# Attention, MoE and MLP in one kernel: token sums tied into the order, weight conversion shifted between blocks, one weight split and one set of weight sums placed elsewhere

## The chip, the cores and the metric

One Trainium2 chip, one core. The metric is the device time of one execution in microseconds; the kernel before takes 698.25 us (median of three runs, 697.82 to 699.86).

## The reference

Three stages follow each other on 1152 tokens of width 512 (2 batches of 576).

```python
scores = scale * q @ k.T + decay, causal          # 2 batches, 8 heads, head size 64
attn   = softmax(scores) @ v                      # -> x, 1152 x 512
p      = domain_probs / (sum + 1e-9)
out    = sum over 4 experts of p[:, e] * (relu(x @ w1[e]) @ w2[e])   # 512 -> 1024 -> 512
h      = out @ w_in;  g = h * sigmoid(1.702 * h)  # 512 -> 2048
result = g @ w_out                                # 2048 -> 512
```

All of it is float32; the MLP's two weights arrive as 64-bit floats.

## The kernel before, in words

**Precision.** Every operand of a product is split into a high part, rounded by ScalarE to the type that TensorE takes, and a low part, the remainder, subtracted by VectorE. A product is three matmuls: high by high, low by high, high by low. So each weight needs a split (`split_w`, line 242: ScalarE rounds on line 71 into `whi`, VectorE subtracts on line 249 into `wlo`), and each result is evacuated from PSUM with a rounding and a subtraction (`evac_l1`, lines 1082 to 1088; `output`, lines 980 to 985, in which VectorE makes `jc`, ScalarE applies relu and rounds to `hh`, and GpSimd subtracts `hl`).

**Units.** The experts are cut into 8 blocks of half an expert, the MLP into 4 blocks (8 to 11). `visits` lists which block is worked on when, over which groups of tokens; `seq` lists the units in order. A unit of kind 1 is a first layer (4 steps), kind 2 a second layer (one step for each tile of 128 tokens), kinds 4 and 5 a second layer of a visit without rest (8 and 2 steps), kinds 3 and 7 are joint first layers in 7 steps. While visits 0 to 6 run, attention is woven in: `pull()` emits a piece of it, and the number of pulls of a step is `n`, worked out from what is due and how many steps are left (line 1404). Visits 7 to 9 (`v_exp` to `v_all`) handle 640 of the tokens for three blocks; visit 10 is `v_all`; visits 11 to 13 (`both_joint`) handle all tokens, 640 of them (`EXP`) in joint units of 320 columns and the other 512 (`REST`) in joint units of 256 columns; visits 14 to 17 are the MLP.

**Joint units.** `emit_joint` (line 961) multiplies two halves of the tokens with two halves of the weights in 7 products of 6 matmuls in place of 8, after Strassen and Winograd. It needs sums of weights (`sum_weights`, line 260: four GpSimd operations on lines 270 to 273 into `sr`; `high_sums` and `low_sums` split them into `sh` and `sl`) and sums of tokens: `sum_tokens` (line 309) for EXP, and `rest_sums` (line 338) for the 512 tokens of REST. The last of the 7 products (s4) adds onto a bank that `third_out` reads first, on VectorE (line 980).

**Token sums of REST.** `rest_sums` is a generator of 44 steps: twice 22, for two halves of the width. 28 are VectorE operations of 128x256 (20 sums on line 362, 8 subtractions on line 355), 8 are ScalarE roundings, 8 are transfers (line 357) from the one buffer `rs` to DRAM. Its scratch lies in an attention pool. Three steps of it are emitted at each step of `seq` from the fourth step of unit (1, 5, 1, 1) on. They name only their data, so the scheduler puts them on the engines as early as these allow.

**Order.** A scheduler orders each engine's instructions by program order among those that are ready in its own estimate of time. `in_turn(fn)` (line 799) ties each instruction that fn emits to come behind the one emitted last on its engine (TensorE, VectorE, ScalarE and GpSimd; not SyncE, which issues most transfers). From visit 7 to 13 `pin_turn` fixes the emitted order on VectorE, ScalarE and GpSimd, and on TensorE where the line `pinned = ...` says so. In a step the order is: matmuls of the step, pulls, token sums, evacuation of the step before (`evac[0]()`), a split that is due, what `place()` puts at that step, conversion.

**place().** `put(u, g, what, ...)` (line 1283) puts an action at step g of unit u. For a visit of `both_joint` the units are, in order: h0 = (3, v, ., EXP[0]); the second layer of REST of the visit before; r0 = (7, v, ., 0); h1 = (3, v, ., EXP[1]); r1 = (7, v, ., 1); l2 = (2, v, ., EXP[0]). The four splits of the second layer's weights ("b") and the weight sums of the next visit are put there by hand.

**Conversion.** `mlp_convert` (line 406) turns an MLP weight from 64-bit to 32-bit floats in 6 steps of the generator: one VectorE operation of 128x512 each (lines 419, 422, 425, 428, 431, 433); the first has a ScalarE operation (line 418) ahead of it, the last is followed by a load (line 400) and a store (line 446) on SyncE. `cv_due` collects a rate at every step of `seq`, and each whole unit of it emits one step of the generator. There are 32 weights, 192 steps.

Of the kernel before, what the change touches and what calls it, by code (L numbers as in the profile page):

```python
# [28 lines left out]
EXP = [NCH + 3, NCH + 4, NCH + 5]  # L29
# [21 lines left out]
def attn_moe_mlp(ctx: ExitStack, tc: tile.TileContext, qk0, qk1, qk2, v0, vp, fg, dp, wa_moe, wb_moe, wa_mlp, wb_mlp, out):  # L51
# [36 lines left out]
    late = {}  # L88
# [67 lines left out]
    v_exp, v_all, v_mlp = len(visits), len(visits) + 3, len(visits) + 7  # L156
    visits += [(b, EXP[:2]) for b in (3, 1, 0)] + [(b, EXP) for b in range(4, NMOE)] + [(b, MLP) for b in range(NMOE, NBLK)]
    joint = [v_ for v_ in range(v_exp, len(visits)) if v_ != v_mlp]
    both_joint = range(v_all + 1, v_mlp)
# [616 lines left out]
    def in_turn(fn, *args):  # L776

        block = nc.cur_bb.bb.instructions
        n, prev = len(block), {}
        for i in block:  # L780
            prev[i.engine] = i
        fn(*args)
        for i in block[n:]:
            if i.engine in turn_engines:
                if i.engine in prev:
                    tc.add_manual_dep(i, prev[i.engine].name,
                                      mybir.DependencyInfo(mybir.DependencyClass.NoSync, mybir.DependencyReason.DATA),
                                      reason="in_turn")
                prev[i.engine] = i
# [496 lines left out]
    def place():  # L1286

        at = {}

        def put(u, g, what, *args):  # L1290
            at.setdefault((u, g), []).append((what, args))

        for v_ in range(v_exp, v_all):
            b, (c1, c2) = visits[v_]
            h0, h1, l2 = (3, v_, b, c1), (3, v_, b, c2), (4, v_, b, c1)
            put(h0, 1, sum_weights, v_ + 1, 0)
            put(h1, 1, sum_weights, v_ + 1, 1)
            for u, m in ((l2, 0), ((5, v_, b, c1), 1)):
                put(u, -0.5, high_sums, v_ + 1, m)
                put(u, 0, low_sums, v_ + 1, m)  # L1300
            first = v_ == v_exp
            places = [(h1, 5), (h1, 6)] + [(l2, i) for i in range(1, 7)]
            if first:
                put((6,) + units[-1], -0.5, high_sums, v_, 1)
                put((6,) + units[-1], 0, low_sums, v_, 1)
                nxt0 = (3, v_ + 1, visits[v_ + 1][0], c1)
                places = [(h0, 0), (h0, 1)] + places + [(nxt0, 0), (nxt0, 1)]
            todo = [("b", v_)] * first + [("a", v_ + 1), ("b", v_ + 1)]
            for (kind, w_, g), (u, i) in zip([(*t, g) for t in todo for g in range(4)], places):
                put(u, i, split_w, kind, w_, g)  # L1310
        for v_ in range(v_all, v_mlp):
            b, (c1, c2, _) = visits[v_]
            h0, h1, l2 = (3, v_, b, c1), (3, v_, b, c2), (2, v_, b, c1)
            more = v_ + 1 in both_joint
            if v_ == v_all:
                mid = (1, v_, b, REST)
                put(h1, 0, load_rest_sums)
                put(h0, 1, sum_weights, v_ + 1, 0)
                put(mid, -0.5, high_sums, v_ + 1, 0)
                put(mid, 0, low_sums, v_ + 1, 0)  # L1320
                put(mid, 1, sum_weights, v_ + 1, 1)
                continue
            r0, r1 = (7, v_, b, 0), (7, v_, b, 1)
            put(r0, -0.5, split_rest)
            put(r0, 5.5, high_sums, v_, 1)
            put(h1, -0.5, low_sums, v_, 1)
            if more:
                put((2, v_ - 1, b - 1, REST), 2, sum_weights, v_ + 1, 0)
                put(h1, 1, sum_weights, v_ + 1, 1)
                put(r1, 6, high_sums, v_ + 1, 0)  # L1330
                put(l2, 0, low_sums, v_ + 1, 0)
            fill = (2, v_ - 1, b - 1, REST)
            for k, (u, i) in enumerate([(fill, 3), (fill, 3), (r0, 1), (r1, 1)]):
                put(u, i, split_w, "b", v_, k)
            for g in range(4):
                put(l2, g, split_w, "a", v_ + 1, g)
        return at
# [11 lines left out]
    late_by = [3]  # L1349
    rest_gen, rest_from = [], seq.index((1,) + units[6])  # L1350
    cv_due = [0]
    in_turn(emit_first, 3, True)
    for i, (kind, v_, b, c) in enumerate(seq):
# [24 lines left out]
        for g in range(n_steps):  # L1378
            if kind in (2, 6):
                split_until("b", v_, range(4))  # L1380
            elif kind not in (4, 5):
                split_until("a", v_, [g] if kind == 1 else range(4))
            if i == 0:
                ev = lambda: None
            elif kind in (3, 7):
                ev = next(j_gen)
            else:
                if kind in (4, 5) and ("b", v_, 2 if kind == 5 or g > 4 else 0) in lo_of:
                    split_rest()
                ev = (emit_l1(v_, b, c, g) if kind == 1 else  # L1390
                      emit_l2_pair(v_, b, c, g) if (kind, c) == (2, REST) and v_ + 1 in both_joint and g >= n_steps - 2 else
                      emit_l2(v_, b, c, g) if kind == 2 else
                      emit_l2(v_, b, c, g + len(tiles(c)) - OVER) if kind == 6 else emit_l2_joint(v_, b, c, g, kind == 5))
            for _ in range(sums_at.get(u, 0)):
                in_turn(next, ts_gen, None)
            if sum_due and kind != 6:
                split_sums_done()
            if kind == 3 and g == 6:
                j_done.add((v_, m))
            n = 0  # L1400
            if nxt:
                j, cc = nxt[0]
                left = sum(steps(*u) for u in seq[i:j]) - g
                n = max(0, -(-(due[cc] - pulled[0]) // left))
                for _ in range(n):
                    pull()
            if rest_gen and not late:
                for _ in range(3 if late_by[0] <= 0 else 0):
                    next(rest_gen[0], None)
                late_by[0] -= 1  # L1410
            rests = []
            for d in split_due[:]:
                d[0] -= 1
                if d[0] == 0:
                    split_due.remove(d)
                    rests.append(split_output(d[1]))
            for what, args in place_at.get((u, g - 0.5), ()):
                what(*args)
            low_now = lows[:]
            lows.clear()  # L1420
            evac[0]()
            for l_, q, h_ in low_now:
                nc.vector.tensor_sub(l_, q, f(h_))
            for r in rests:
                r()
            evac[0] = ev
            split_next()
            if len(split_q) > 4:
                split_next()
            for what, args in place_at.get((u, g), ()):  # L1430
                what(*args)
            if v_ + 1 < len(visits) and not v_exp <= v_ < v_all:
                if u == last_l1[v_] and kind == 1:
                    split_q.append(("a", v_ + 1, g))
                if u == last_l2[v_] and g == n_steps - 1 and v_ + 1 != v_exp and v_ + 1 not in both_joint:
                    split_q.extend(("b", v_ + 1, k) for k in range(4))
            if late:

                if sums_at.get(u, 0) < 2:
                    if v_ in both_joint and v_ + 1 in both_joint or v_ + 1 == v_mlp and c != REST or v_ == v_all and kind == 2 and c == REST:  # L1440
                        rate = 0 if kind != 2 else 11 / 4 if c == REST else 2.25
                    elif v_ == v_all:
                        rate = {3: 0, 1: 1.75, 2: 3.5}[kind]
                    else:
                        rate = (1.25 if kind == 4 else 0) if v_ < v_all else 1.4 if v_ == v_all else 1.75
                    cv_due[0] += rate * (4 / n_steps) if rate != 11 / 4 else 3 * (g < 3)
                while cv_due[0] >= 1:
                    in_turn(next, cv_gen[0], None)
                    cv_due[0] -= 1
                load_owed()  # L1450
            if v_ >= v_exp:
                pinned = v_ > v_mlp and (kind, c, g) == (3, MLP[0], 6) or v_ >= v_mlp and (kind, c, g) in ((2, MLP[2], 1), (2, MLP[2], 2)) or v_ > v_mlp and (kind, c, g) == (3, MLP[1], 1) or v_ < v_all or v_ == v_all and kind == 3 or v_all <= v_ < v_mlp and u in pin_units
                (pin_engines.add if pinned else pin_engines.discard)(nc.tensor.engine)
                pin_turn()
            else:
                pin_from[1] = len(nc.cur_bb.bb.instructions)
# [58 lines left out]
```

## Time and profile before

| | |
|---|---|
| median of 3 runs | 698.25 us |
| profiled execution, its own time | 700.31 us |
| its span, first to last instruction | 698.6 us |
| busy: TensorE, weight loads, VectorE, ScalarE, GpSimd | 98%, 86%, 76%, 51%, 34% |
| share of the chain that ended last: TensorE, VectorE, ScalarE, GpSimd | 81%, 7%, 4%, 3% |
| granted TensorE clock, mean | 0.998 |

"Busy" counts the time in which an engine had an instruction in work; matmuls overlap, so TensorE can be busy and yet not be at its peak. The chain that ended last is followed back from the last instruction: at each point to what released it. A timeline row reads: start, duration, engine, line, operation, tile written <- tiles read, shape, number of instructions merged, and in brackets the idle time of the engine before it and what ended that.

### The profile page before, as it was taken

Reading aid. Unit: us, or ns where it says so; the run is one execution under the profiler, and the core shown is the slowest. Engines: PE = TensorE matmul, PEld = TensorE weight load, DVE = VectorE, ACT = ScalarE, POOL = GpSimd, SP = SyncE. Lnnn points to the kernel's source line nnn. Section 1 sums busy time; section 2 is a strip of 40 time slices with the busy share of each in tenths; the row PEclk is TensorE's granted clock in tenths of the full one; section 3 lists DMA queues with packets and bytes.
Section 4 is the critical chain, followed back from the end, with each engine's and each line's share of the span. In section 5 each row is a group of like instructions: output and inputs, shape, how many; then the busy total and the mean of one; then the engine's idle time right before and its main releaser. Section 6 shows DMA issues by size and latency. Waiting matters only on the chain.

```text
span 698.6 us, 11080 instructions
## 1 busy us (share of the span) xinstructions
PE 682.5 (98%) x3936; PEld 601.0 (86%) x3937; DVE 532.9 (76%) x1097; ACT 353.4 (51%) x821; POOL 236.1 (34%) x286
## 2 busy tenths in 40 slices
PE   8999989999999999999999999999999999999997
PEld 4797878888988988888888898898899898998986
DVE  6897799776559688686886687666789989998632
ACT  5778667776533635644246235253357354453520
POOL 6886466443133454443035233123003210220000
PEclk9999999999999999999999999999999999999999
DMA  7687636342412143154621423223331544441012
GB/s 258 221 300 257 248 135 229 120 141 70 114 59 63 59 151 106 34 163 166 197 76 38 144 76 101 84 73 106 121 106 50 160 153 122 154 162 61 1 46 90
DMA packets 41063, 87.59 MB, mean 125 GB/s; under 512 B 3720, under 2 KB 5776, under 8 KB 40752
## 3 DMA queue, kind: packets, MB, share of 16 engines
q1 hardware_dynamic: 40680, 84.75, 37.5%
q0 software_dynamic: 288, 2.10, 0.8%
q8 instruction: 31, 0.51, 0.3%
q14 instruction: 24, 0.20, 0.1%
q10 hardware_dynamic: 40, 0.04, 0.0%
HBM read 73.98 MB, written 12.88 MB: 124 GB/s over the span
## 4 chain that ended last, share of the span: by engine, by line
PE 81%; DVE 7%; ACT 4%; POOL 3%; issue 2%; DMA 1%; SPq 0%; DVEq 0%; POOLq 0%; ACTq 0%
PE m L1099 38%; PE m L974 16%; PE m L934 16%; PE s L652 4%; PE x L756 3%; PE t L726 3%; DVE wlo L249 1%; ACT jc L983 1%; DVE jc L980 1%; ACT hh L71 1%; DMA wst<-in_wb_moe_dram 1%; POOL hl L985 1%; ACT sh L71 1%; ACT whi L71 1%; DVE acc L1143 1%
## 5 line engine op out<-in xcount | busy, mean ns | idle before, releaser
L1099 PE MATMUL m<-whi,hh 128*128 128x512 f32 x392 | 109.6, 393 | 2.0 <-DVE sm L705 2.0
L1099 PE MATMUL m<-wlo,hh 128*128 128x512 f32 x392 | 109.5, 393 | 0.0
L1099 PE MATMUL m<-whi,hl 128*128 128x512 f32 x392 | 108.1, 391 | 0.0
L249 DVE TENSOR_TENSOR wlo<-wst,whi 128x512 fp32r<-128x512 f32 x132 | 100.3, 773 | 8.6 <-ACT whi L71 8.0
L985 POOL TENSOR_TENSOR hl<-jc,hh 128x320 fp32r<-128x320 f32 (+1 forms) x60 | 52.6, 879 | 149.9 <-ACT hh L71 147.3
L71 ACT ACTIVATE whi<-wst 128x512 fp32r<-128x512 f32 x136 | 80.7, 624 | 31.1 <-PE m L1099 15.8
L1099 PEld LDWEIGHTS m<-wlo,hh 128*128 128x128 f32 x392 | 73.7, 189 | 15.4
L1099 PEld LDWEIGHTS m<-whi,hl 128*128 128x128 f32 x392 | 73.8, 189 | 15.4
L1099 PEld LDWEIGHTS m<-whi,hh 128*128 128x128 f32 x392 | 72.0, 188 | 14.9 <-DVE sm L705 2.2
L270 POOL TENSOR_TENSOR sr<-wst 128x256 f32<-128x256 f32 x20 | 18.1, 904 | 155.8 <-DMA wst<-wm 69.0
L708 POOL TENSOR_SCALAR e<-e,sm 128x128 f32<-128x128 f32 (+4 forms) x72 | 45.3, 641 | 62.2 <-DVE sm L706 36.2
L983 ACT ACTIVATE jc<-jc 128x320 f32<-128x320 f32 (+1 forms) x60 | 27.0, 450 | 63.4 <-DVE jc L980 63.0
L1143 DVE SCALAR_TENSOR_TENSOR acc<-m,dpn,acc 128x512 f32<-128x512 f32 x63 | 46.5, 744 | 9.8 <-PE m L1099 9.6
L698 ACT ACTIVATE e<-e,mx 128x128 f32<-128x128 f32 (+4 forms) x72 | 41.8, 581 | 19.3 <-DVE mx L682 17.7
L934 PE MATMUL m<-xh,whi 128*128 128x256 f32 (+2 forms) x256 | 51.4, 316 | 0.0
L934 PE MATMUL m<-xh,wlo 128*128 128x256 f32 (+2 forms) x256 | 51.4, 314 | 0.0
L934 PE MATMUL m<-xl,whi 128*128 128x256 f32 (+2 forms) x256 | 50.9, 315 | 0.0
L934 PEld LDWEIGHTS m<-xh,whi 128*128 128x128 f32 x256 | 41.4, 189 | 1.4
L934 PEld LDWEIGHTS m<-xh,wlo 128*128 128x128 f32 x256 | 41.7, 189 | 0.9
L1082 ACT ACTIVATE m<-m 128x384 f32<-128x384 f32 x48 | 23.0, 480 | 37.9 <-DVE m L980 36.2
L934 PEld LDWEIGHTS m<-xl,whi 128*128 128x128 f32 x256 | 41.1, 189 | 0.7
L1012 ACT ACTIVATE u<-m 128x320 f32<-128x320 f32 (+2 forms) x26 | 11.2, 432 | 53.7 <-PE m L974 53.7
(173 smaller groups left out, 1516.5 us busy)
## 6 DMA issues: line engine op xcount, KB each, us to landing
wst<-in_wa_moe_dram SPq DMA_DIRECT2D x28, 512.0 KB, 4.1
wst<-in_wb_moe_dram SPq DMA_DIRECT2D x28, 512.0 KB, 3.8
mst<-in_wa_mlp_dram SPq DMA_DIRECT2D x16, 512.0 KB, 4.2
wm<-wf SPq DMA_DIRECT2D x32, 256.0 KB, 4.0
mst<-in_wb_mlp_dram SPq DMA_DIRECT2D x16, 512.0 KB, 4.0
wst<-wm SPq DMA_DIRECT2D x16, 512.0 KB, 4.0
cb<-cumd SPq DMA_DIRECT2D x16, 256.0 KB, 5.2
qr<-in_qk_dram SPq DMA_DIRECT2D x8, 384.0 KB, 5.1
```

The costliest lines, as they stand in the source:

```text
L71: return nc.scalar.activation(out=out, in_=in_, func=AF.Copy)
L249: (nc.gpsimd if v_ == 0 and kind == 'a' and g < 4 else nc.vector).tensor_sub(lf, raw, f(hf))
L652: nc.tensor.matmul(pt[:, :z - a], lhsT=lr[i][0], rhs=lr[i][1], start=i == 0 and not (both and pt is not bank), stop=i == n - 1, skip_group ...
L698: nc.scalar.activation(out=e[:, off:off + w], in_=e[:, off:off + w], func=AF.Exp, scale=-1.0, bias=mx, accum_out=sm[:, 0, k:k + 1])
L708: nc.gpsimd.tensor_scalar(out=e[:, off:off + w], in0=e[:, off:off + w], scalar1=sm[:, 0, i:i + 1], scalar2=1.0, op0=ALU.mult, op1=ALU.mult)
L934: nc.tensor.matmul(p[:, :n], lhsT=w[:, k, :], rhs=x[c][:, k, :], start=(j == 0 and k == 0), stop=(j == 2 and k == 3))
L974: nc.tensor.matmul(p[:, :WN], lhsT=w[a][:, k, :], rhs=x[z][:, k, :], start=start and j == 0 and k == 0, stop=stop and j == 2 and k == 1, s ...
L983: nc.scalar.activation(out=r, in_=r, func=AF.Relu)
L985: nc.gpsimd.tensor_sub(hl[:, g, :], r, f(hh[:, g, :]))
L1082: nc.scalar.activation(out=p[:, :n], in_=p[:, :n], func=AF.Gelu_apprx_sigmoid)
L1099: nc.tensor.matmul(p, lhsT=h_tile(v_, b, c, j, x, k), rhs=wb[v_, k][w].rearrange("p a c -> p (a c)"), start=i == 0 and k == 0, stop=i == 2 ...
L1143: nc.vector.scalar_tensor_tensor(out=a, in0=p, scalar=d, in1=a, op0=ALU.mult, op1=ALU.add)
```

## The change

Token sums of REST: where three steps of `rest_sums` stood in a step of `seq`, two now stand among the pulls of that step (behind pull n // 3 and behind pull 2n // 3, so both behind the first where n is 1, and none where n is 0) and one behind the evacuation; each is called through `in_turn`. Conversion: the rate in the second-layer units of visits 7 to 9 goes from 1.25 to 0.75; in h0 of visits 11 to 13 one step is emitted at g = 0 and one at g = 2. In `place()`, for visits 11 to 13: the fourth "b" split goes from r1, step 1, to h1, step 2; the second half of the next visit's weight sums goes from h1, step 1, to r1, step 5.

```diff
             if more:
                 put((2, v_ - 1, b - 1, REST), 2, sum_weights, v_ + 1, 0)
-                put(h1, 1, sum_weights, v_ + 1, 1)
+                put(r1, 5, sum_weights, v_ + 1, 1)
                 put(r1, 6, high_sums, v_ + 1, 0)
                 put(l2, 0, low_sums, v_ + 1, 0)
             fill = (2, v_ - 1, b - 1, REST)
-            for k, (u, i) in enumerate([(fill, 3), (fill, 3), (r0, 1), (r1, 1)]):
+            for k, (u, i) in enumerate([(fill, 3), (fill, 3), (r0, 1), (h1, 2)]):
                 put(u, i, split_w, "b", v_, k)
...
                 n = max(0, -(-(due[cc] - pulled[0]) // left))
-                for _ in range(n):
+                if rest_gen and not late:
+                    late_by[0] -= 1
+                spread = (n // 3, 2 * n // 3) if late_by[0] < 0 and not late else ()
+                for k in range(n):
                     pull()
-            if rest_gen and not late:
-                for _ in range(3 if late_by[0] <= 0 else 0):
-                    next(rest_gen[0], None)
-                late_by[0] -= 1
+                    for _ in range(spread.count(k)):
+                        in_turn(next, rest_gen[0], None)
             rests = []
...
             evac[0]()
+            if late_by[0] < 0 and not late:
+                in_turn(next, rest_gen[0], None)
             for l_, q, h_ in low_now:
...
-                        rate = (1.25 if kind == 4 else 0) if v_ < v_all else 1.4 if v_ == v_all else 1.75
+                        rate = (0.75 if kind == 4 else 0) if v_ < v_all else 1.4 if v_ == v_all else 1.75
+                    if kind == 3 and v_ in both_joint and c == EXP[0]:
+                        cv_due[0] += g in (0, 2)
                     cv_due[0] += rate * (4 / n_steps) if rate != 11 / 4 else 3 * (g < 3)
```

The emptying of the generator before the last first layer of visit 6 (`for _ in rest_gen[0]: pass`, not through `in_turn`) is as it was; it was empty by then.

## Rows read from the trace of the kernel before

**Rows 1.** The page's busy time of the engines, share of the span.

```profile
PE 682.5 (98%) x3936; PEld 601.0 (86%) x3937; DVE 532.9 (76%) x1097; ACT 353.4 (51%) x821; POOL 236.1 (34%) x286
```

**Rows 2.** TensorE's wait for VectorE, 57 to 200 us: line, releaser, us in total, times, longest.

```profile
PE m L1099 <- DVE sm L705: 2.0, 1, 2.0
```

**Rows 3.** TensorE's waits, 235 to 320 us, then 320 to 480 us.

```profile
PE m L974 <- DVE jc L980: 1.9, 3, 0.8
...
PE m L974 <- DVE jc L980: 3.1, 3, 1.3
```

**Rows 4.** VectorE's timeline ahead of TensorE's wait at 92 to 94 us.

```profile
92.62 1.62 DVE L355 TENSOR_TENSOR rs<-rsb,rs 128x256 fp32r<-128x256 f32 x1
94.16 0.41 DVE L1088 SCALAR_TENSOR_TENSOR hl<-m,hh 128x256 fp32r<-128x256 f32 x1
```

**Rows 5.** Stretches: us, busy (instructions) by engine, granted clock, DMA share, GB/s.

```profile
94.00:100.00 6.00, 5.37 (x17) 4.40 (x18) 5.38 (x25) 2.66 (x10) 4.50 (x8) 0.72 0.53 186
57.00:128.00 71.00, 67.28 (x459) 57.78 (x457) 60.78 (x164) 47.91 (x134) 40.54 (x49) 0.98 0.62 219
160.00:200.00 40.00, 40.00 (x280) 34.52 (x279) 21.00 (x62) 22.59 (x62) 9.57 (x15) 1.00 0.29 93
200.00:225.00 25.00, 25.00 (x129) 22.55 (x128) 22.94 (x32) 8.17 (x15) 9.05 (x8) 1.00 0.14 43
243.00:254.00 11.00, 10.89 (x61) 9.68 (x59) 10.99 (x18) 3.94 (x8) 4.53 (x5) 1.00 0.72 228
```

**Rows 6.** The tile rs: duration ns min/median/max, first and last start.

```profile
L357 SPq DMA_DIRECT2D tsd<-rs x8: 360/374/419, 66.8 to 127.8; - x8
L355 DVE TENSOR_TENSOR rs<-rsb,rs x4: 414/606/1618, 92.6 to 127.4; 128x256 fp32r<-128x256 f32 x4
...
DMA to landing us min/median/max: 2.1/2.1/3.6
```

**Rows 7.** VectorE's timeline, first and last token sum of EXP in visit 6.

```profile
201.33 0.82 DVE L330 TENSOR_TENSOR tr<-xh 128x640 f32<-128x640 f32 x1
...
222.08 1.30 DVE L325 TENSOR_TENSOR tl<-tr,th 128x640 fp32r<-128x640 f32 x1 [0.81 <-ACT th L71]
```

**Rows 8.** TensorE's timeline, where the fourth product of h0, visit 7, begins.

```profile
225.33 0.45 PE L974 MATMUL m<-th,sh 128*128 128x320 f32 x2
```

**Rows 9.** VectorE's conversion operations by line, 241 to 309 us: cheapest and dearest.

```profile
L431 DVE SCALAR_TENSOR_TENSOR cvd<-mst,cvt 128x512 f32<-128x512 uint32 x2 | 2.6, 1300 | 0.0
...
L428 DVE TENSOR_SCALAR cvt<-wf 128x512 uint32<-128x512 uint32 x2 | 0.8, 414 | 0.0
```

**Rows 10.** VectorE's timeline in h0 of visits 11 and 12.

```profile
347.17 0.49 DVE L980 TENSOR_TENSOR jc<-m,u 128x320 f32<-128x320 f32 x1
...
393.18 0.49 DVE L1017 TENSOR_TENSOR u<-m,u 128x320 f32<-128x320 f32 x1 [1.07 <-PE m L974]
```

**Rows 11.** TensorE's timeline, s4 of h0, visit 11.

```profile
347.96 0.46 PE L974 MATMUL m<-xh,sh 128*128 128x320 f32 x2
```

**Rows 12.** GpSimd's timeline in h1 of visit 11.

```profile
368.96 0.75 POOL L270 TENSOR_TENSOR sr<-wst 128x256 f32<-128x256 f32 x1
...
371.88 1.71 POOL L985 TENSOR_TENSOR hl<-jc,hh 128x320 fp32r<-128x320 f32 x2
```

**Rows 13.** VectorE's timeline in h1 and r1 of visit 11.

```profile
369.44 0.49 DVE L980 TENSOR_TENSOR jc<-m,u 128x320 f32<-128x320 f32 x1 [0.30 <-PE m L974]
...
372.79 0.49 DVE L980 TENSOR_TENSOR jc<-m,u 128x320 f32<-128x320 f32 x1 [2.46 <-POOL hl L985]
...
374.85 0.95 DVE L249 TENSOR_TENSOR wlo<-wst,whi 128x512 fp32r<-128x512 f32 x1 [0.83 <-ACT whi L71]
```

**Rows 14.** TensorE's timeline, s4 of h1 and r1, visit 11.

```profile
370.06 0.48 PE L974 MATMUL m<-xh,sh 128*128 128x320 f32 x2
...
375.04 0.40 PE L974 MATMUL m<-tsl,whi 128*128 128x256 f32 x2
376.71 0.50 PE L974 MATMUL m<-xh,sh 128*128 128x256 f32 x2 [1.27 <-DVE jc L980]
```

## The prediction, written before the changed kernel ran

> **What bounds the kernel now.** I read the engines' busy time first: TensorE 98%, VectorE 76% [rows 1]. TensorE is the bound, and an edit that adds no matmul can win only what TensorE waits. Its waits are few: between 57 and 200 us one of 2.0 us for VectorE [rows 2], between 235 and 480 us six, of 1.9 and 3.1 us together, all for a `jc` of VectorE [rows 3]. The timelines show what VectorE does just before each.
>
> At 92 us it subtracts a token sum of REST for 1.62 us, and only then reaches the evacuation on line 1088 [rows 4]. The profile names a small operation right behind that evacuation as releaser [rows 2]; I read this as the evacuation, since the matmuls that wait need a free bank. Afterwards the granted clock is 0.72 on the mean of 6 us [rows 5]: a part of that stretch ran at the lower of the two levels, 1.2 of 2.4 GHz.
>
> The first three of the six waits lie in h0 of visits 8 to 10. VectorE is busy 10.99 of 11.00 us ahead of the first [rows 5], so any operation taken from that stretch comes off the wait. The other three are s4 of r1 in visits 11 to 13. In visit 11 GpSimd makes four weight sums from 368.96 on, and the evacuations `hl` of h1 stand behind them until 371.88 [rows 12]; VectorE's next `jc` waits 2.46 us for the first of these, and later the fourth split's subtraction takes 0.95 us between two links of the same chain [rows 13]; s4 waits 1.27 us [rows 14].
>
> **The change part by part.** Token sums. Of 44 steps the old code emitted three at each of 15 steps of `seq`, all of them. The pulls fall out as n = 1 in 5 of these 15 steps and n = 0 in 10 (32 units of attention, due at 32 and 35 pulls), so the new code emits 5 x 3 + 10 x 1 = 25, and the remaining 19 in one go before the last first layer of visit 6. They hold 17 and 11 of the 28 VectorE operations. None can now run before its place in the order, so all leave the stretch from 57 to 128 us, where VectorE is busy 60.78 of 71 us, for 160 to 200 us, where it is busy 21.00 of 40, and for 200 to 225 us, where it is busy 22.94 of 25 [rows 5].
>
> What goes: the 2.0 us wait, and what the clock took, (1 - 0.72) x 6 = 1.7 us; together 3.7. Next in line there is the key split on VectorE beside GpSimd, which without the sums has its evacuation right behind it; I let the whole 3.7 go, bounds 0 and 3.7.
>
> What it adds: 17 operations of 0.41 us at least [rows 6] are 7 us in a stretch with 19 us idle; tied behind what was emitted before, each can hold a later evacuation by one operation. I take nothing, with the 19 idle us as cover; without it, at most the 7. The 19 late steps matter more. The buffer `rs` is single, so each of their four rounds is a rounding (about the 0.41 us of the subtraction), a subtraction of 0.41 to 0.61, an issue of 0.37 on SyncE and a landing of 2.1 before the next rounding may write [rows 6]: about 3.4 us. Starting at 202 us, the last VectorE operation comes after three rounds and 0.8 us more, near 213. And `sum_tokens`, called through `in_turn`, ties its first operation behind the last VectorE instruction emitted: that last sum. So the EXP sums, which began at 201.33 [rows 7], begin near 213. They are 14 VectorE operations of 0.82 us or more [rows 7], 11.5 us, and some 3 us of roundings between: done near 227.5. Evacuations and splits that stood between them may move into the idle time before 213. The fourth product of h0 needs the last of them at 225.33 [rows 8]. That is 2.2 us late; TensorE has second-layer tiles of the visit before to pull ahead. I take a loss of 1.0 us, bounds 0 and 10.
>
> Conversion. Each of visits 7 to 9 loses two of five steps (rate 0.75 x 4 = 3 for 5). An operation took 0.41 to 1.30 us there [rows 9], so two are 0.8 to 2.6 us. Each wait is 0.8 at most [rows 3]; I let the 1.9 us go, bounds 1.0 and 1.9. Next late would be the ScalarE rounding behind s4, which is off TensorE's way. The six steps, one whole weight, come back as two in h0 of visits 11 to 13. In visit 11 `jc` starts at 347.17 and runs 0.49 [rows 10], and s4 starts at 347.96 [rows 11]: 0.3 us to spare. Two operations of at least 0.41 ahead of it overrun this by 0.5; at the dearest in rows 9, by 2.3. In visit 12 VectorE idles 1.07 us before its first sum [rows 10], which covers them, and I take visit 13 alike. Cost 0.5 us, bounds 0 and 2.3. The ScalarE operation of a new weight stands in front of h0's first copy; its load and the store on SyncE come six steps later for the same weight, and no MLP weight is due before visit 14, by which all steps are made up.
>
> Weight sums and fourth split. Out of h1's GpSimd queue go four operations, 368.96 to 371.88 [rows 12]; out of r1's VectorE queue goes 0.95 us [rows 13]. Either is near the 1.27 us wait, so the 3.1 us of three visits go (in visit 13 there are no weight sums, only the split). Bounds 1.5 and 3.1. In r1 at step 5 the sums stand ahead of two `hl` of REST, which are needed after the next h0 and the sums' rounding in the next r0: nothing. Their reads of the raw weights end before the splits of l2 do, so no buffer is held longer; the "b" buffer comes free earlier for SyncE's next load.
>
> The fourth split now stands in h1, where a `jc` starts at 369.44, ends 0.49 later, and s4 starts at 370.06 [rows 13, 14]: 0.13 us to spare. A split of 0.95 at most, part of it in VectorE's idle 0.30 us [rows 13], leaves 0 to 0.5 per visit; I take 0.3, in all 0.9 us (bounds 0 and 2.9, the whole 0.95 in each).
>
> Each of the six waits costs a little more than it is listed with: from 375.04 to 376.71 are 1.67 us, and the listed 1.27 takes the pair at 375.04 as lasting its full 0.40, which in a stream overlaps with the next pair by about half [rows 14]. I add some 0.17 for each, 1.0 us in all.
>
> At this place a row and a rule differ. With GpSimd beside it a subtraction of 0.41 us took 1.62 [rows 6]. The weight sums now lie beside l2, where VectorE converts and splits; I count nothing for it, since VectorE idles 1.07 us behind that l2 [rows 10]. The Trainium skill (SBUF — State Buffer, "SBUF: two separate sides") has the port pair that VectorE and GpSimd share as an exclusive lock, held for a whole instruction, which speaks against this edit; by it the sum would be that of the fourth rival.
>
> Sum: -3.7 + 1.0 - 1.9 + 0.5 - 3.1 + 0.9 - 1.0 = -7.3 us. The profiled execution took 700.31 us, 2.06 above the median; the terms are differences within it, and I take them off the median: 698.25 - 7.3 = 690.95, about 691.0 us.
>
> **The rivals.** (1) Attention gives nothing. Something else holds that evacuation (the scheduler orders this whole stretch anew), or the late sums cost what the early ones did: -2.7 of the sum falls away, 693.7 us. For it: VectorE stays over 60% busy there without the sums; against: 28 operations leave it.
> (2) The fourth split only moves its wait from r1 to h1: 2.0 us more, 693.0 us. For it the 0.13 us to spare, against it the 0.30 idle [rows 13].
> (3) Slower: the late chain passes on one to one. The rounds take a landing of up to 3.6 us [rows 6], 4.2 us a round with waits in the queues; the last token sum comes near 215.5, the EXP sums start 14 us late and nothing is pulled ahead. Beyond the 2 us between 223.4 [rows 7] and 225.33 [rows 8], TensorE stands 12 us before h0 of visit 7 and loses 1.7 to the clock as it did at 92 us: 691.0 - 1.0 + 13.7 = 703.7, about 703 us. It decides if the first EXP sum begins after about 210 us and the other VectorE work does not move ahead of it. For it: the code's tie and single buffer; against it: 19 of 40 us idle before.
> (4) GpSimd's four sums hold VectorE by their whole length, 2.92 us [rows 12], in l2 of visits 11 and 12. Some 1.07 us behind and as much between the sums of h0 cover it; 0.7 us reach s4 twice: 692.4 us.
>
> **How the numbers follow.** Chances: forecast 0.50, attention nothing 0.22, split moved 0.10, late chain 0.12, port 0.06. A measurement can tell 0.3%, 2.1 us, from no change. All but the late chain are faster by more; that one may end between 698 and 710, and I put 0.09 of it beyond 700.4 and 0.03 within. Rivals 1 and 2 with the worst bounds together come within 0.3% (0.03). So 0.85 faster, 0.06 same, 0.09 slower. The range: all gains without a cost are 698.25 - 9.7 = 688.5; I go to 686.5, since a new order may also take small waits of attention that I don't count. Upward rivals 1 and 2 and one lesser cost give 697.0. The late chain stays outside.
>
> **What would show it.** Right: no row of token sums before 155 us; no wait of TensorE at 92 us and no lowered clock there; no waits for `jc` over 0.3 us in h0 of visits 8 to 10 and in r1 of 11 to 13; `sr` of the second half beside l2; a wait of at most 0.5 us before s4 of h1, and of h0 in visit 11. Wrong: the first EXP sum after 210 us with TensorE waiting before 230; a clock under 1 anywhere in 200 to 260; a new wait over 1 us in attention; or waits for `jc` that merely moved to h1.

## The result, and the profile after

The changed kernel takes 703.07 us (median of four runs, 702.49 to 704.16) beside 698.06 us for the kernel before on the same chip (697.82 to 699.86): a ratio of 1.0068, interval 1.0047 to 1.0089. It is slower by 0.7%; the forecast was 691.0 us, and the third rival, with 703 us at a chance of 0.12, is the one whose mechanism and time came. The profiled execution after took 702.49 us (span 700.8), the one before 700.31 (span 698.6); the first lies under its median and the second over it, so the two traces show 2.2 of the 5.0 us. One execution below, the traced one of experiment 1, ran at a mean granted clock of 0.557 throughout and took 1124.87 us; it is left out of that ratio.

The engines' busy time on the page, to be laid beside [rows 1], says nothing of where they went:

```profile
PE 685.0 (98%) x3936; PEld 601.5 (86%) x3937; DVE 533.1 (76%) x1097; ACT 355.0 (51%) x821; POOL 238.1 (34%) x286
```

TensorE's waits do: changed kernel, stretches 57 to 200, 200 to 235, 235 to 320 and 320 to 480 us (line, releaser, us in total, times, longest), to be read beside [rows 2, 3].

```profile
PE t L726 <- POOL e L708: 1.4, 1, 1.4
PE x L756 <- ACT ph L71: 0.3, 1, 0.3
...
PE m L974 <- ACT th L71: 4.4, 1, 4.4
PE m L974 <- DVE tl L325: 0.3, 1, 0.3
...
PE m L974 <- DVE jc L980: 0.9, 1, 0.9
PE m L974 <- DVE sl L303: 0.3, 1, 0.3
...
PE m L974 <- DVE jc L980: 1.2, 3, 0.4
```

The wait of 2.0 us at 92 us is gone, as forecast; so are the three waits in h0 of visits 8 to 10, and the three of 3.1 us in r1 have become three of 1.2 us together. In their place stands one of 4.4 us, for the token sum `th` of EXP; the 0.9 us below 320 is new too, in visit 7. TensorE's timeline there:

```profile
217.17 1.07 PE L1099 MATMUL m<-whi,hl 128*128 128x512 f32 x4
218.07 0.30 PE L974 MATMUL m<-xl,whi 128*128 128x320 f32 x1
222.79 0.85 PE L974 MATMUL m<-th,sh 128*128 128x320 f32 x2 [4.42 <-ACT th L71]
223.98 1.91 PE L1099 MATMUL m<-whi,hh 128*128 128x512 f32 x4
```

The second product of h0 stands at the head, and four second-layer matmuls that stand behind it in the order (223.98) run only after it. The clock follows; stretches in the columns of [rows 5], the granted clock third from the end:

```profile
222.00:224.00 2.00, 1.21 (x5) 1.21 (x6) 1.22 (x2) 0.74 (x1) 1.28 (x2) 0.72 0.00 0
224.00:226.00 2.00, 2.00 (x6) 1.61 (x6) 1.60 (x3) 0.33 (x1) 0.00 (x0) 0.50 0.53 202
226.00:228.00 2.00, 2.00 (x9) 1.61 (x9) 1.56 (x2) 0.41 (x1) 0.65 (x1) 0.93 0.16 60
```

0.50 is the lower level, 1.2 GHz; the three rows lose 0.56 + 1.0 + 0.14 = 1.7 us. So the chain costs 4.4 + 1.7 us, and the waits of 0.3, 0.9 and 0.3 us that follow in the same visit 1.5 more: 7.6 us in visit 7, where the kernel before had no wait listed.

This is not the whole of it. The last `jc` of visit 7, before and after:

```profile
240.28 0.48 DVE L980 TENSOR_TENSOR jc<-m,u 128x320 f32<-128x320 f32 x1
```

```profile
246.76 0.48 DVE L980 TENSOR_TENSOR jc<-m,u 128x320 f32<-128x320 f32 x1
```

It comes 6.5 us later. From 57 us to there the waits and the clock add up to 9.3 us after (the 7.6, and 1.4 and 0.3 of attention) and to 5.4 us before (2.0 and the clock's 1.7 at 92 us, and 1.7 of attention), 3.9 us apart. The other 2.6 us stand in no listed wait of TensorE and in no stretch of lowered clock, and where they go is open.

Why `th` is late is in two timelines and the view of a tile. VectorE, with the last token sum of REST, the first of EXP and the second and last `tl`:

```profile
201.68 0.75 DVE L1143 SCALAR_TENSOR_TENSOR acc<-m,dpn,acc 128x512 f32<-128x512 f32 x1 [1.98 <-PE m L1099]
...
207.22 0.43 DVE L355 TENSOR_TENSOR rs<-rsb,rs 128x256 fp32r<-128x256 f32 x1 [1.37 <-ACT rs L71]
...
213.90 0.41 DVE L355 TENSOR_TENSOR rs<-rsb,rs 128x256 fp32r<-128x256 f32 x1
214.23 0.81 DVE L330 TENSOR_TENSOR tr<-xh 128x640 f32<-128x640 f32 x1
...
222.78 1.27 DVE L325 TENSOR_TENSOR tl<-tr,th 128x640 fp32r<-128x640 f32 x1 [0.80 <-ACT th L71]
...
231.37 1.29 DVE L325 TENSOR_TENSOR tl<-tr,th 128x640 fp32r<-128x640 f32 x1
```

ScalarE, with the roundings of REST and the first two of EXP:

```profile
206.77 0.42 ACT L71 ACTIVATE rs<-rsb 128x256 fp32r<-128x256 f32 x1 [3.17 <-DMA tsd<-rs]
...
213.33 0.42 ACT L71 ACTIVATE rs<-rsb 128x256 fp32r<-128x256 f32 x1 [0.74 <-DVE wlo L249]
...
216.80 0.74 ACT L71 ACTIVATE th<-tr 128x640 fp32r<-128x640 f32 x1 [2.01 <-DVE tr L330]
222.01 0.74 ACT L71 ACTIVATE th<-tr 128x640 fp32r<-128x640 f32 x1 [4.46 <-DVE tr L330]
```

The tile `rs`, as in [rows 6]:

```profile
L355 DVE TENSOR_TENSOR rs<-rsb,rs x4: 408/425/426, 182.7 to 213.9; 128x256 fp32r<-128x256 f32 x4
...
DMA to landing us min/median/max: 2.1/2.4/5.2
```

A rounding waits 3.17 us for the transfer to leave the one buffer, VectorE's subtraction waits for the rounding, the last subtraction comes at 213.90, and the first EXP sum right behind it, 12.9 us later than in [rows 7]. (The last rounding, at 213.33, is listed behind VectorE's `wlo`: there the written order, and not only the buffer, may have held it.)

In h1 of visit 11 the fourth split now stands in the chain of [rows 13]. VectorE, and TensorE's s4:

```profile
372.88 0.81 DVE L249 TENSOR_TENSOR wlo<-wst,whi 128x512 fp32r<-128x512 f32 x1 [0.57 <-ACT whi L71]
...
374.22 0.49 DVE L980 TENSOR_TENSOR jc<-m,u 128x320 f32<-128x320 f32 x1
```

```profile
374.76 0.56 PE L974 MATMUL m<-xh,sh 128*128 128x320 f32 x2 [0.40 <-DVE jc L980]
```

### The profile page after: what moved, and what is told of

It reads as the page before. It is cut to its first block, busy times and chain, and to the rows that moved or that the text cites. A ratio compares the mean times of both kernels' runs of the same rounds, so it can differ in the third digit from the quotient of the medians.

```text
span 700.8 us, 11093 instructions
## 1 busy us (share of the span) xinstructions
PE 685.0 (98%) x3936; PEld 601.5 (86%) x3937; DVE 533.1 (76%) x1097; ACT 355.0 (51%) x821; POOL 238.1 (34%) x286
## 5 line engine op out<-in xcount | busy, mean ns | idle before, releaser
L698 ACT ACTIVATE e<-e,mx 128x128 f32<-128x128 f32 (+4 forms) x72 | 41.6, 580 | 12.9 <-DVE mx L682 12.3
```

What stands on the lines that cost most here:

```text
L698: nc.scalar.activation(out=e[:, off:off + w], in_=e[:, off:off + w], func=AF.Exp, scale=-1.0, bias=mx, accum_out=sm[:, 0, k:k + 1])
```

## The experiments

All ratios are against the kernel before on the same chip, where its median was 700.0 to 700.5 us in these three groups of runs; a ratio is formed from the single executions and can differ by up to 0.2% from the quotient of the medians. Expectations in us are on the scale of 698.1 us.

**1. The sums' edit alone.** The changed kernel without its other edits:

```diff
-                put(r1, 5, sum_weights, v_ + 1, 1)
+                put(h1, 1, sum_weights, v_ + 1, 1)
...
-            for k, (u, i) in enumerate([(fill, 3), (fill, 3), (r0, 1), (h1, 2)]):
+            for k, (u, i) in enumerate([(fill, 3), (fill, 3), (r0, 1), (r1, 1)]):
...
-                        rate = (0.75 if kind == 4 else 0) if v_ < v_all else 1.4 if v_ == v_all else 1.75
-                    if kind == 3 and v_ in both_joint and c == EXP[0]:
-                        cv_due[0] += g in (0, 2)
+                        rate = (1.25 if kind == 4 else 0) if v_ < v_all else 1.4 if v_ == v_all else 1.75
```

> The kernel before with the token sums' edit alone. Theory (late chain: the EXP sums are tied behind the last token sum of REST, begin at 214 us in place of 201, and TensorE stands for them): the loss is all here, and the other two edits gave back about 1.6 us each (the waits of 1.9 and 3.1 us gone, some 0.3 and 1.5 back), so 703.1 + 3.2 = 706.3 us (704.5 to 708), with a wait for th of about 4.4 us near 218 us, a granted clock of about 0.8 behind it, and no wait at 92 us. Rival (the token sums are about even, 4 us of wait gone at 92 us against 4.4 at 218, and the loss of the medians lies with the conversion or with the split and weight sums): 698 to 700 us.

Measured: ratio 1.0119 (1.0092 to 1.0147), from three executions of 706.8, 706.9 and 709.6 us; 706.3 on 698.1 is 1.0117. All of the loss is in the sums, and more than the result shows. The wait and the clock that were expected are not tested by this run; experiments 2 and 3 bear on them.

**2. The other edits, without the sums'.** The changed kernel with the sums as before:

```diff
-                if rest_gen and not late:
-                    late_by[0] -= 1
-                spread = (n // 3, 2 * n // 3) if late_by[0] < 0 and not late else ()
-                for k in range(n):
+                for _ in range(n):
                     pull()
-                    for _ in range(spread.count(k)):
-                        in_turn(next, rest_gen[0], None)
+            if rest_gen and not late:
+                for _ in range(3 if late_by[0] <= 0 else 0):
+                    next(rest_gen[0], None)
+                late_by[0] -= 1
...
-            if late_by[0] < 0 and not late:
-                in_turn(next, rest_gen[0], None)
```

> The changed kernel with the token sums as before: conversion, fourth split and weight sums changed. Theory: these gain what the waits say, 698.1 - 3.2 = 694.9 us (693.5 to 696.5); the wait at 92 us of 2.0 is there, none for th near 218. Rival: they lose, 698.5 us or more.

Measured: 0.9938 (0.9917 to 0.9958). The other edits are worth 4.3 us; 3.2 was expected, within the interval. The 2.0 us wait at 92 us is back, and TensorE has no wait between 200 and 235 us.

**3. All sums emitted in time.** Nothing is left to be emptied out before the last first layer:

```diff
             if late_by[0] < 0 and not late:
-                in_turn(next, rest_gen[0], None)
+                for _ in range(1 if n else 3):
+                    in_turn(next, rest_gen[0], None)
```

> The changed kernel with three tied steps of the token sums at each step of seq also where no pull falls in it, so that all 44 stand in the order before the last first layer of visit 6 and none is emptied out at once. Theory: the first EXP sum comes some 4 to 6 us earlier, near 209 us, each us of it comes off the wait near 218 and the clock's loss behind it goes too: 703.1 - 4.4 - 1.9 = 696.8 us (695 to 699). Rival 1 (what costs is that the sums are tied at all, each holding an evacuation of attention): no better, 703 us or more, with new waits between 160 and 205 us. Rival 2 (the single buffer and its transfers pace the sums however early they stand in the order): first EXP sum still behind 212 us, 701 to 703 us.

Measured: 0.9978 (0.9964 to 0.9993), against an expected 696.8 on 698.1, 0.9981. VectorE's last subtraction of REST and first EXP sum, and TensorE's waits from 200 to 235 us:

```profile
208.26 0.42 DVE L355 TENSOR_TENSOR rs<-rsb,rs 128x256 fp32r<-128x256 f32 x1 [0.77 <-ACT rs L71]
208.60 0.82 DVE L330 TENSOR_TENSOR tr<-xh 128x640 f32<-128x640 f32 x1
```

```profile
PE m L974 <- ACT th L71: 1.5, 1, 1.5
PE m L974 <- DVE tl L325: 0.5, 1, 0.5
```

The subtraction and the sum come 5.6 us sooner, and the wait of 4.4 us is 1.5: the theory holds in this and in the time. The clock's loss did not go in the traced execution, whose granted clock is 0.74 and 0.83 in the two stretches of 4 us from 228 us on, 1.7 us again. No new wait stands between 160 and 200 us and the time is better, so rival 1 falls as it was written; whether ties cost something is for runs 5 and 10.

**4. The first EXP sum untied.**

```diff
             for _ in range(sums_at.get(u, 0)):
-                in_turn(next, ts_gen, None)
+                if exp_first.pop() if exp_first else False:
+                    next(ts_gen, None)
+                else:
+                    in_turn(next, ts_gen, None)
...
-    late_by = [3]
+    late_by, exp_first = [3], [True]
```

> The changed kernel with the first operation of the EXP sums not tied behind the last token sum of REST. Theory (the tie on VectorE): the first three EXP sums and the weights' sl, 3.8 us of VectorE, move into the idle time between 199 and 213 us, the wait near 218 us shrinks by about as much and most of the clock's loss goes: 703.1 - 3.8 - 1.5 = 697.8 us (696 to 700). Rival (the tie on ScalarE: the first rounding th still stands behind the last rounding of REST, which waits for its transfer): the wait stays over 3 us, 701.5 to 703.5 us.

Measured: 1.0022 (1.0012 to 1.0033), between the theory (697.8 on 698.1, 0.9996) and the rival (1.005 to 1.008). ScalarE, then TensorE:

```profile
217.69 0.42 ACT L71 ACTIVATE rs<-rsb 128x256 fp32r<-128x256 f32 x1 [1.17 <-DMA tsd<-rs]
218.02 0.72 ACT L71 ACTIVATE th<-tr 128x640 fp32r<-128x640 f32 x1
```

```profile
222.02 0.63 PE L974 MATMUL m<-th,sh 128*128 128x320 f32 x2 [2.44 <-ACT th L71]
```

The first sums did move ahead, but the first rounding `th` comes right behind the last of REST, which waits for its transfer: both are right in part. The chain passes through two engines, and undoing its tie on one of them gives back some 3.2 of the 5.3 us that the theory had.

**5. Begun one unit sooner, all tied.** On top of experiment 3:

```diff
-    rest_gen, rest_from = [], seq.index((1,) + units[6])
+    rest_gen, rest_from = [], seq.index((1,) + units[5])
```

> The changed kernel with the token sums still tied, three at every step of seq, but begun one unit (six steps of seq) sooner, so that all 44 stand well ahead of the EXP sums. Theory (late chain): the EXP sums begin near 201 us as before the change, no wait for th near 218 us, no wait at 92 us, so the 3.7 us that the prediction counted for that wait and the clock behind it come on top of what the run without the sums' edit gave (0.9938 of the time before): 694.6 - 3.7 = 690.9 on the scale of that call, a ratio of 0.987 to 0.990. Rival 1 (early sums, tied, hold attention's evacuations wherever they stand): waits of 1 to 4 us in all between 130 and 180 us, ratio 0.992 to 0.998. Rival 2 (a late chain is only moved: the EXP sums still come behind 206 us, since VectorE falls behind all through attention): ratio about 0.995.

Measured: 0.9953 (0.9935 to 0.9971): the theory is missed, and the ratio lies where rivals 1 and 2 had put it. Neither is met as it was written: the EXP sums begin at 205.6 us and not behind 206, and the new wait of 1.1 us ends at 193.5 and not before 180. The tile `rs`, the EXP sums, TensorE's wait between 130 and 200 us, and the last `jc` of visit 7:

```profile
L355 DVE TENSOR_TENSOR rs<-rsb,rs x4: 419/640/921, 161.5 to 198.2; 128x256 fp32r<-128x256 f32 x4
```

```profile
L330 DVE TENSOR_TENSOR tr<-xh x2: 812/816/819, 205.6 to 221.4; 128x640 f32<-128x640 f32 x2
```

```profile
PE m L934 <- DVE acc L1143: 1.1, 1, 1.1
```

```profile
241.66 0.48 DVE L980 TENSOR_TENSOR jc<-m,u 128x320 f32<-128x320 f32 x1
```

The last subtraction of REST comes at 198.2, though begun some 21 us sooner than in the changed kernel (161.5 for 182.7, by the first of this row), and EXP starts 4.3 us after [rows 7]. TensorE has no wait for `th` even so.

**6. Two tied steps at a time, begun two units sooner.** `units[4]`, and one sum among the pulls and one behind the evacuation:

```diff
-                spread = (n // 3, 2 * n // 3) if late_by[0] < 0 and not late else ()
+                spread = (n // 2,) if late_by[0] < 0 and not late else ()
...
-                in_turn(next, rest_gen[0], None)
+                for _ in range(1 if n else 2):
+                    in_turn(next, rest_gen[0], None)
```

> The same begun two units sooner and with two tied sums at a step in place of three, a thinner spread. Theory: also no wait near 218 us; ratio 0.987 to 0.991, equal to the run with three a step within 0.2%. Rival (the stretch from 120 to 160 us, in which VectorE is busier, 70 to 87%, passes on every tied operation to an evacuation): 0.5 to 2 us dearer than three a step begun one unit later.

Measured: 0.9956 (0.9940 to 0.9973), the same as experiment 5: its theory's equality holds, its level does not. Its last subtraction of REST starts at 198.6 us and its first EXP sum at 205.0, as there.

**7 and 8. Split and weight sums apart.** Both without the sums' edit. In 7 the fourth split is back in r1, in 8 the weight sums are back in h1:

```diff
-            for k, (u, i) in enumerate([(fill, 3), (fill, 3), (r0, 1), (h1, 2)]):
+            for k, (u, i) in enumerate([(fill, 3), (fill, 3), (r0, 1), (r1, 1)]):
```

```diff
-                put(r1, 5, sum_weights, v_ + 1, 1)
+                put(h1, 1, sum_weights, v_ + 1, 1)
```

> The run without the sums' edit, with the fourth split back in r1: conversion and weight sums changed alone. Theory (the four GpSimd operations in h1 made the whole of r1's wait, the split stood in VectorE's idle time): the three waits of 0.4 us in h1 go and r1 waits at most 0.3 us each, 0.5 to 1.5 us faster than the run without the sums' edit: ratio 0.992 to 0.9933. Rival (either alone is half of r1's wait): waits of 0.6 us or more in r1 of visits 11 and 12, ratio 0.994 to 0.996.

> The run without the sums' edit, with the weight sums back in h1: conversion and fourth split changed alone. Theory (GpSimd makes r1's wait): r1 of visits 11 and 12 waits 0.9 to 1.3 us still, and h1 0.4 us each: ratio 0.9955 to 0.998. Rival (the split made it): as the run without the sums' edit, 0.993 to 0.9945.

Measured: 0.9935 (0.9917 to 0.9954) and 0.9934 (0.9913 to 0.9954), both as experiment 2. s4 of r1 in 7, s4 of h1 in 8, and VectorE's next `jc` in 8:

```profile
373.38 0.51 PE L974 MATMUL m<-xh,sh 128*128 128x256 f32 x2 [0.41 <-DVE jc L980]
```

```profile
368.95 0.56 PE L974 MATMUL m<-xh,sh 128*128 128x320 f32 x2 [0.40 <-DVE jc L980]
```

```profile
371.54 0.49 DVE L980 TENSOR_TENSOR jc<-m,u 128x320 f32<-128x320 f32 x1 [2.25 <-PE m L974]
```

In 7 some 0.4 us stays in r1 and none is in h1; in 8, with GpSimd's four sums still in h1, r1 does not wait at all. So the theory of 7 is met by half in the waits, with a ratio just above its 0.9933, and that of 8 falls for its rival: either edit alone takes some 0.85 us off the wait of 1.27 [rows 14], and the two together no more than one.

**9, 10 and 12. One tie in place of 44.** Without the sums' edit, only the first of the 44 steps is tied; the others follow from its data and go where the scheduler puts them. They begin two units sooner than before (9, `units[4]`), one (10, `units[5]`) or as before (12, `units[6]`). The edit of run 10, against experiment 2:

```diff
-    late_by = [3]
-    rest_gen, rest_from = [], seq.index((1,) + units[6])
+    late_by, rest_first = [3], [True]
+
+    def apply_(fn, *args):
+        fn(*args)
+
+    rest_gen, rest_from = [], seq.index((1,) + units[5])
...
-                    next(rest_gen[0], None)
+                    (in_turn if rest_first else apply_)(next, rest_gen[0], None)
+                    rest_first.clear()
```

> The run without the sums' edit (conversion, split and weight sums changed), with the token sums begun two units sooner in the order and only their first operation tied; the other 43 steps, three to a step of seq, are left to the scheduler. Theory (only two things count: that no sum stands ahead of the evacuation at 92 us, and that the last is done before the EXP sums are due at 201): the 92 us wait goes with its 1.7 us of clock and nothing comes in its place, 0.9938 - 3.7 / 700 = ratio 0.9885 (0.987 to 0.990). Rival (attention has no room for the sums after 92 us either: each of them ends up ahead of some evacuation or rounding): the wait at 92 us goes and others of 2 to 4 us come between 100 and 200 us, ratio 0.992 to 0.9955.

> The same begun one unit sooner than in the kernel before. Theory: as the run begun two units sooner, 0.987 to 0.991. Rival (the room ends before 201 us: the sums crowd 170 to 200 us as in the run with all tied and begun one unit sooner): 0.9945 to 0.9965, waits of 2 us between 180 and 235 us.

> The same begun where the kernel before begins, again with the first operation alone tied. Theory (lateness is what costs, not the ties): as the run with all 44 tied in the same steps, 0.9965 to 0.999, first EXP sum near 208 us, TensorE waiting 1.5 to 2.5 us near 228. Rival (the ties, by which each sum holds what stands behind it, cost): 0.992 to 0.995, no wait near 228 us.

Measured: 0.9941 (0.9920 to 0.9962), **0.9910 (0.9892 to 0.9927)** and 0.9981 (0.9967 to 0.9996). Run 10 beats both kernels: 693.53 us beside 700.16 (medians). It meets the upper end of its theory's range, but not the equality with run 9. Its tile `rs`, first EXP sum and last `jc` of visit 7, and its only wait of TensorE between 57 and 320 us:

```profile
L355 DVE TENSOR_TENSOR rs<-rsb,rs x4: 408/417/880, 155.2 to 180.5; 128x256 fp32r<-128x256 f32 x4
```

```profile
198.60 0.82 DVE L330 TENSOR_TENSOR tr<-xh 128x640 f32<-128x640 f32 x1
...
237.55 0.48 DVE L980 TENSOR_TENSOR jc<-m,u 128x320 f32<-128x320 f32 x1
```

```profile
PE t L726 <- POOL e L708: 1.4, 1, 1.4
```

The sums fit between 150 and 181 us without a listed wait of TensorE. Run 9 puts the chain at 119 to 158 us, and there it meets attention (waits between 130 and 200 us):

```profile
PE x L756 <- ACT ph L71: 0.8, 1, 0.8
PE s L652 <- DVE mx L682: 0.7, 1, 0.7
```

Its rival holds by the ratio, with waits of 1.5 us where it had 2 to 4. Run 12 begins where the changed kernel begins and is as slow as experiment 3, which has all 44 tied from the same place. Its last sum of REST is at 206.8 us, the first of EXP at 204.4 (near 208 was expected), and TensorE waits 2.0 us between 200 and 235 us, though for `tl` and a `jc`, not for `th`: lateness costs, with one tie or with 44. Against run 10, which has one tie, run 5 at the same begin loses 0.4%, and the intervals do not overlap: there the ties cost. By what is shown only in part. The chain of run 5 ends 17.7 us later (198.2 for 180.5), its EXP sums begin 7.0 us later, and by the last `jc` of visit 7 it is 4.1 us behind; the waits listed from 57 us to there are 2.8 us for 1.4, and the other 2.7 us are in no wait. The two runs also differ in where within a step of `seq` the sums stand.

**11. The conversion's edit alone.**

```diff
-                        rate = (1.25 if kind == 4 else 0) if v_ < v_all else 1.4 if v_ == v_all else 1.75
+                        rate = (0.75 if kind == 4 else 0) if v_ < v_all else 1.4 if v_ == v_all else 1.75
+                    if kind == 3 and v_ in both_joint and c == EXP[0]:
+                        cv_due[0] += g in (0, 2)
```

> The kernel before with the conversion's edit alone. Theory: the three waits of 1.9 us in h0 of visits 8 to 10 go, 0.3 us comes in visit 11: 1.6 to 2.0 us, ratio 0.997 to 0.9978; the waits of 3.1 us in r1 stay. Rival (they were hidden by what follows, or return in visits 11 to 13): 0.999 to 1.001.

Measured: 0.9959 (0.9943 to 0.9975), 2.9 us (1.8 to 4.0) where 1.6 to 2.0 were expected. The traces, 3.8 us apart, show 2.4 of conversion behind 1.4 that the clock at 92 us took in one of them and not in the other (last section). No wait for `jc` is left between 235 and 320 us; those of r1 stay:

```profile
372.94 0.51 PE L974 MATMUL m<-xh,sh 128*128 128x256 f32 x2 [1.25 <-DVE jc L980]
```

## Why the prediction was wrong

**The step that failed** is the term of +1.0 us for the late sums, "TensorE has second-layer tiles of the visit before to pull ahead". The steps up to it came true: the last 11 VectorE operations of REST run from 202.79 us on, the roundings of the four rounds begin 3.1 to 3.6 us apart (203.20, 206.77, 209.84 and 213.33) for a forecast of 3.4, and the EXP sums began at 214.23 us for a forecast "near 213". What it did to TensorE was worked out wrongly, in two ways: in place of 1.0 us it waits 4.4 and loses up to 1.7 to the clock.

First, I set the last EXP sum, forecast for 227.5 us, against the fourth product at 225.33, 2.2 us. The product that stood was the second one, whose `th` is the second split: rounded from 222.01 on, when TensorE had come to it at 218.4. A chain that starts 13 us late has to be laid against every point at which something of it is due, not against its end.

Second, the cover was not there. The order on TensorE is written beforehand; tiles that stand behind the waiting product did not pass it, as the 1.91 us of second layer at 223.98 show; VectorE had written the last `wlo` ahead of them by 213.3 us. The Trainium skill (PSUM — Partial Sum Buffer, "Engine vs sequencer instructions") says that matmuls start and complete in program order; the trace agrees, no matmul begins between 218.07 and 222.79. Nor did evacuations and splits fill VectorE's idle time before 213 us, as I had supposed they may: some ran between the sums, but from 200 to 214 us it is busy 9.95 of 14 us, and its gaps of 1.98 and 1.37 us are waits for TensorE and for ScalarE's `rs`, with the chain in the same queue.

The third rival had the mechanism and its sign: its condition, a first EXP sum after 210 us, was met. Its price of 13.7 us was worked out as a wait of 12 and a clock of 1.7. In the trace it is a wait of 4.4, a clock of 1.7 and 1.5 of waits behind. Set against run 10, which differs from the changed kernel only in the begin, the place and the ties of the sums, it is 1.0068 / 0.9910, 1.6% or 11 us. The traced spans (700.8 and 692.0) show 8.8 of these, and 7.9 can be read as waits and clock up to the end of visit 7 (9.3 for 1.4); the rest I can't place. That the time came out at its 703 us is luck: the price was some 2.7 us too high, and the other gains were too high by 2.0.

**The term of -3.7 us** (the wait at 92 us and the clock behind it) was right in the trace and too large on the median: from experiment 2 to run 10, with that wait gone and no other in its place, 0.28% or 2.0 us are gained, though the intervals leave room from 0 to some 4. (The waits for `jc` of run 10 in h1 are 1.6 us, for 1.2 there.) The clock's 1.7 us of the profiled execution was taken off a median that need not have had it (below). Rival 1, that attention gives nothing, holds for the runs with all sums tied (5 and 6), not for run 10.

**Conversion.** -1.9 + 0.5, with half a microsecond for restarts, came to -1.9; run 11 measured -2.9 us (-1.8 to -4.0), its trace -2.4. The waits went, and the 0.5 us in h0 of visit 11 shows as no listed wait.

**Weight sums and fourth split.** -3.1 + 0.9 - 0.5 came to -2.7; from run 11 to experiment 2 it is 0.9959 to 0.9938, -1.5 us, with intervals that overlap. In the trace 3.1 us became 1.2, where 0.9 was forecast. The step "either is near the 1.27 us wait, so the 3.1 us go" was right in that the second edit adds nothing to the first, and too large in that either leaves 0.4 us of each wait (7 and 8). Rival 2 (the wait moves whole to h1) and rival 4 (GpSimd holds VectorE in l2) show no wait of their size.

Together: all terms but the late chain gave, in run 10, 0.9910 x 698.25 = 692.0 us; without its 1.0 for the chain the forecast was 690.0. That this is near is in part luck, since the terms are off by 1.7 and 1.2 us one way and by 1.0 the other. A chance of 0.12 for the late chain was too low: the code showed the tie and the single buffer, the rounds' pace put the EXP sums past the rival's own threshold of 210 us, and only its price was open.

## What to carry to other kernels

Tying work into an order to keep it out of a busy stretch also gives it an earliest time: whatever is tied behind it inherits the delay, on every engine of the chain. Find where each piece of the delayed chain is due, piece by piece, and count on an in-order engine's later work as cover only if it stands ahead of the wait in the written order. Here one tie, at the head of the chain and placed so that the chain ran from 150 to 181 us and ended 18 us ahead of the EXP sums, did what 44 were meant to do.

## What the hardware showed that was not expected

Five traces have the wait of TensorE at 92 us, 2.0 us in each. The lower clock followed it in three (the kernel before and runs 2 and 8, a granted clock of 0.72 from 94 to 100 us) and not in two (7 and 11, 1.00). Stretch 94 to 100 us in experiment 2, then in run 11 (columns as in [rows 5]):

```profile
94.00:100.00 6.00, 4.73 (x15) 3.94 (x16) 5.72 (x24) 2.66 (x10) 4.46 (x8) 0.72 0.58 189
```

```profile
94.00:100.00 6.00, 5.22 (x27) 4.53 (x28) 5.42 (x25) 3.32 (x14) 4.46 (x8) 1.00 0.61 187
```

What it costs is in TensorE's timeline, the second four matmuls behind the wait in the kernel before and in run 11:

```profile
95.81 1.91 PE L1099 MATMUL m<-wlo,hh 128*128 128x512 f32 x4
```

```profile
95.81 1.07 PE L1099 MATMUL m<-wlo,hh 128*128 128x512 f32 x4
```

The same four matmuls `whi,hl` further on start at 102.39 in the first and at 100.96 in the second: 1.4 us, and the two stay so far apart up to the end of visit 7 (last `jc` at 240.28 and 238.90). Among 52 executions of the kernel before in the three groups, the 22 with a mean clock of 0.998 or less have medians of 700.3, 701.4 and 701.2 us, the others 699.0, 699.5 and 699.7: some 1.5 us that come and go with nothing changed in the kernel. Where in those executions the clock fell isn't recorded. One traced execution may hold such a microsecond or not, and a term read from it should be halved or left as a bound.

The other finding is on GpSimd beside VectorE, in the changed kernel's late sums:

```profile
222.63 0.73 POOL L273 TENSOR_TENSOR sr<-wst,sr 128x256 f32<-128x256 f32 x1
```

```profile
226.44 0.83 DVE L325 TENSOR_TENSOR tl<-tr,th 128x640 fp32r<-128x640 f32 x1 [0.81 <-ACT th L71]
```

VectorE's subtraction that begins 0.15 us after GpSimd's, at 222.78, takes 1.27 us; the same subtraction at 226.44, with no GpSimd operation beside it, takes 0.83. The Trainium skill (SBUF — State Buffer, "SBUF: two separate sides") has the port pair of the two as an exclusive lock, kept by the one that starts first; this pair agrees: GpSimd keeps its 0.73, and VectorE is longer by 0.44, so a late chain is also slowed by whatever it now lies beside. The subtraction of 1.62 us at 92.62 [rows 4], of which the prediction said that a row and a rule differ, is such a pair too; GpSimd began 0.13 us ahead of it, and it ends 0.28 us behind GpSimd's end:

```profile
92.49 1.47 POOL L578 TENSOR_TENSOR ks<-kq,ks 64x576 fp32r<-64x576 f32 x1
```
